# Token weights turned by blocks of rows, and a new order of all steps, in a fused attention and mixing kernel

## The chip, the cores and the metric

The kernel runs on one core of a Trainium2 chip. The core has five engines, each with its own stream of instructions that it works through in order: TensorE (PE; its weight loads are shown apart as PEld), VectorE (DVE), ScalarE (ACT), GpSimd (POOL) and SyncE (SP), which here issues all DMA transfers. Engines wait for each other by semaphores. The metric is device time in microseconds (us) of one execution. The kernel before takes 235.92 us, the median of 3 runs (235.21 to 237.58).

## The reference: what is computed

A block of attention is followed by a block that mixes tokens and channels. Batch 8, heads 8, 576 tokens, 64 features per head; all inputs and the output are float32.

```python
# attention, for each batch and head
q_d, k_d, v_d = means of q, k, v over groups of 4 tokens          # 144 tokens
out_d = softmax(q_d @ k_d.T / 8) @ v_d                             # coarse, all to all
scores = where(|i - j| < 4, q @ k.T / 8, -1e9)                     # local, a band
x = repeat(out_d, 4) + softmax(scores) @ v                         # heads side by side: [8, 576, 512]

# mixing
theta = x @ w_theta
zr, zi = x * cos(theta), x * sin(theta)
y[b] = w_tok_r @ zr[b] + w_tok_i @ zi[b]                           # over the 576 tokens
u = x + y
out = u + maximum(u @ w_ch, 0)
```

## The kernel before, in words

All work is in bfloat16 on the chip, with sums in float32 in PSUM, whose eight banks are one tile `PS`. For each of the 8 batches the steps are, with the two-letter words by which the code names them:

- Loads of q and k (`lq`, `lk`, four pairs of heads each), cast to bfloat16 (`cq`, `ck`, L296), turned on TensorE (`tp`, L303) and evicted from PSUM (`ev`, L316) to `qT` and `kT`. Sums over four tokens give `qd` and `kd` (L322 on VectorE; L330 with L333 or L336 on GpSimd). v comes in windows of 64 tokens (`lv`, `lw`) and is cast (`cv`, L396); v of batch 0 is loaded in rows, cast and turned on the chip (`l1`, `c1`, `t1`, `e1`, `x1`).
- Coarse attention: scores `sd`, exponentials `ed` (L437), product with the means of v `nd`, normalisation `xn` (L457, L458), turn `xd` and copy `xc` (L470) to `xdT`.
- Local attention in units of windows: scores `ps` (L482), exponentials `ex` (L490), a mask `mk` (L501) on VectorE or GpSimd, product with v `po` (L511), normalisation `nm` (L519, L520), turn `xt` (L533), and the sum with the coarse part `xa` (L541), which gives `xT`.
- Mixing: `th` (L552) makes theta for 128 tokens, `cs` (L557, L558) its cosine and sine on ScalarE, `xm` turns x, and `zz` (L616) multiplies x by both to make `z`; the last 64 tokens go another way (`tt`, `ct`, `zt`, `zp`, `zc`, L586). `mx` (L632) is the token mixing, 8 groups of 9 products with a row of 288 columns of `WT`; `ua` (L637) adds x and frees the bank. `ch` (L662) is the channel product, `rl` (L667) its addition and `st` the store.

The token weights must be turned once, at the start, before batch 0 can be mixed. `WT` holds nine pieces of 128 rows (source tokens) by 576 columns (target tokens). `lb` loads nine blocks of rows (four of `w_tok_r`, one that holds the last 64 rows of both, four of `w_tok_i`), `cb` (L261) casts each into a place of `uT`, which is not yet in use, `wp` (L273) turns on TensorE what belongs to one of the nine pieces, from five blocks of one matrix, and `wc` (L278) copies the piece, 576 columns, to `WT`. A piece needs all blocks of its matrix, so the first turn waits for the last block of that matrix.

The order is written out by hand: `ORDER` is one list of words. The first two letters name the step, of which the next instance in a fixed sequence is taken; the third says which engine does it (`v`, `a`, `g`) or which banks or which of the 16 staging places `st` it uses. Each engine gets its instructions in the order of this list, and a chain of no-wait dependencies (`pin`) keeps it so; the engines still drift against each other. `wm` words are dummy products on zeros, placed in the start, and `te` and `ts` load ScalarE's table for exponentials or sines. All transfers stand in one queue, on SP.

## Time and profile before

| | us |
|---|---|
| median of 3 runs (lowest, highest) | 235.92 (235.21, 237.58) |
| span of the profiled execution, first to last instruction | 232.1 |
| median less this span | 3.8 |
| TensorE busy | 220.7 |
| VectorE busy | 191.8 |
| ScalarE busy | 156.1 |
| GpSimd busy | 135.5 |

The profiled execution is shown by its span alone; what lies around the span, the start and the end of the execution, is taken as the difference to the median. Rows of a timeline show start, length, engine, line, operation, output and inputs with their shape, and a count where like instructions follow each other. Rows of a group show the line, engine, operation, tiles, shape and count, then the busy time in us and the mean of one in ns, then the engine's idle time just before them and what ended it. Rows of waits show who waited for whom: us in total, times, and the longest. A matmul's record lasts until its result is out, though the next has begun by then, so TensorE's busy time overstates its work.

The DMA queue and the granted clock in 40 slices of the span, in tenths, for the whole of it:

```
PEclk9999999999999999999999999999999999999998
DMA  6999989999999899989606895899957766556676
```

### The profile page before, as it was taken

The page shows a single profiled execution, that of the slowest core. Times are in us where ns is not written, and L with a number is a line of the kernel's source. Part 1 is how long each engine was busy: PE and PEld are TensorE (multiplying, and loading weights), DVE is VectorE, ACT ScalarE, POOL GpSimd, SP SyncE. Part 2 cuts the span into 40 slices and gives each one's busy share as a digit, 9 for nine tenths or more (in the row PEclk, how much of TensorE's full clock was granted, in tenths as well). Part 3 has the DMA queues.
Part 4 walks back from the last instruction along what each step waited for, and adds up shares of the span by engine and source line. Part 5 has one row for each costly group of instructions (what it writes and reads, how often), then busy time and mean ns, then how long its engine had stood idle before and what let it go on. Part 6 is the DMA issues. An engine that isn't in the chain of part 4 may idle for free.

```text
span 232.1 us, 9462 instructions
## 1 busy us (share of the span) xinstructions
PE 220.7 (95%) x3986; PEld 153.2 (66%) x3986; DVE 191.8 (83%) x365; ACT 156.1 (67%) x241; POOL 135.5 (58%) x179
## 2 busy tenths in 40 slices
PE   7998899999998999999999999999999998999991
PEld 2665678777776765776768766676676563767750
DVE  6699999989997988868997997799889967567572
ACT  3359999799877989867976979857766591620000
POOL 7468989869999656897472837767386510000000
PEclk9999999999999999999999999999999999999998
DMA  6999989999999899989606895899957766556676
GB/s 204 382 392 390 298 134 252 365 263 193 264 263 195 224 290 208 203 209 210 174 3 178 226 234 147 293 249 173 153 122 189 144 138 100 154 126 182 138 235 217
DMA packets 76795, 49.41 MB, mean 213 GB/s; under 512 B 61136, under 2 KB 61392, under 8 KB 76752
## 3 DMA queue, kind: packets, MB, share of 16 engines
q1 hardware_dynamic: 76752, 48.81, 84.6%
q8 instruction: 31, 0.51, 1.1%
q14 instruction: 12, 0.10, 0.2%
HBM read 33.98 MB, written 9.44 MB: 187 GB/s over the span
## 4 chain that ended last, share of the span: by engine, by line
PE 72%; DVE 12%; DMA 5%; SPq 3%; issue 3%; ACT 2%; DVEq 0%
PE PS L632 24%; PE PS L662 10%; PE PS L552 9%; PE PS L303 5%; PE PS L755 4%; PE PS L511 3%; DVE xT L541 3%; DMA out_dram<-osb 2%; DVE pm L501 2%; PE PS L591 2%; PE PS L482 2%; DMA st<-xT 2%; SPq L641 2%; PE PS L533 2%; DVE uT L637 2%
## 5 line engine op out<-in xcount | busy, mean ns | idle before, releaser
L632 PE MATMUL PS<-WT,z 128*128 128x288 bf16 x576 | 77.9, 286 | 1.7 <-issue 1.7
L632 PEld LDWEIGHTS <-z 128*128 128x128 bf16 x576 | 53.8, 98 | 17.5 <-issue 2.8
L637 DVE TENSOR_TENSOR uT<-PS,xT 128x288 bf16<-128x288 f32 x64 | 28.1, 450 | 11.4 <-PE PS L632 11.1
L552 PE MATMUL PS<-wth,xT 128*128 128x512 bf16 x128 | 32.3, 380 | 0.7 <-DVE xT L541 0.7
L557 ACT ACTIVATE cs<-PS,pihc 128x512 bf16<-128x512 f32 x32 | 22.3, 696 | 15.1 <-PE PS L552 9.9
L662 PE MATMUL PS<-wch,uT 128*128 128x512 bf16 (+1 forms) x132 | 30.6, 373 | 0.0
L520 DVE TENSOR_TENSOR tmp<-PS,rl 128x512 bf16<-128x512 f32 x40 | 27.7, 692 | 1.4
L541 DVE TENSOR_TENSOR xT<-PS,xdT 128x928 bf16<-128x928 f32 (+1 forms) x24 | 22.7, 952 | 3.4 <-PE PS L533 3.1
L490 ACT ACTIVATE pm<-PS 128x1024 bf16<-128x1024 f32 (+1 forms) x24 | 20.4, 877 | 7.0 <-PE PS L482 2.7
L501 POOL TENSOR_TENSOR pm<-pm,band 128x1024 bf16<-128x1024 bf16 (+1 forms) x13 | 22.2, 1709 | 2.9 <-ACT pm L490 2.9
L667 DVE SCALAR_TENSOR_TENSOR osb<-PS,ur 128x512 f32<-128x512 f32 (+1 forms) x33 | 21.8, 669 | 2.4 <-PE PS L662 1.6
L330 POOL TENSOR_TENSOR two<-kT 128x580 f32<-128x580 bf16 x15 | 17.5, 1163 | 6.1 <-ACT kT L316 5.2
L296 POOL CAST q_tm<-st 128x576 bf16<-128x576 f32 x22 | 14.4, 664 | 10.8 <-DMA st<-in_q_dram 10.8
L662 PEld LDWEIGHTS <-uT 128*128 128x128 bf16 x132 | 12.2, 98 | 12.2 <-issue 0.3
L558 ACT ACTIVATE cs<-PS 128x512 bf16<-128x512 f32 x32 | 19.4, 605 | 0.0
L330 POOL TENSOR_TENSOR two<-qT 128x576 f32<-128x576 bf16 x11 | 12.8, 1167 | 10.5 <-ACT qT L316 7.1
L552 PEld LDWEIGHTS <-xT 128*128 128x128 bf16 x128 | 11.2, 98 | 10.7 <-issue 1.3
L616 DVE TENSOR_TENSOR z<-PS,cs 128x1024 bf16<-128x1024 bf16 x24 | 16.2, 685 | 1.9 <-PE PS L591 0.9
L437 ACT ACTIVATE pd<-PS 128x864 bf16<-128x864 f32 x16 | 14.1, 889 | 5.2 <-PE PS L426 5.2
L761 ACT ACT_TABLE_LOAD x13 | 16.7, 1283 | 0.2
L296 POOL CAST k_tm<-st 128x576 bf16<-128x576 f32 x21 | 14.4, 695 | 1.4 <-DMA st<-in_k_dram 1.4
L396 POOL CAST v_w<-st 128x512 bf16<-128x512 f32 x21 | 13.3, 653 | 1.3 <-DMA st<-in_v_dram 1.2
(119 smaller groups left out, 419.3 us busy)
## 6 DMA issues: line engine op xcount, KB each, us to landing
st<-in_q_dram SPq DMA_DIRECT2D x32, 288.0 KB, 6.3
st<-in_k_dram SPq DMA_DIRECT2D x32, 288.0 KB, 6.0
st<-in_v_dram SPq DMA_DIRECT2D x70, 128.0 KB, 4.7
out_dram<-osb SPq DMA_DIRECT2D x31, 256.0 KB, 2.9
out_dram<-osb SPq DMA_DIRECT2D x10, 128.0 KB, 2.4
st<-in_v_dram SPq DMA_DIRECT2D x4, 288.0 KB, 3.7
st<-in_moe_w_tok_r_dram SPq DMA_DIRECT2D x4, 288.0 KB, 6.2
st<-in_moe_w_tok_i_dram SPq DMA_DIRECT2D x4, 288.0 KB, 7.2
```

Of the source, the lines that this page charges most:

```text
L296: COPY[w](out=to[:, r, :], in_=of[:, r, :])
L330: nc.gpsimd.tensor_tensor(out=t, in0=src[:, :, 0:2], in1=src[:, :, 2:4], op=ALU.add)
L490: nc.scalar.activation(out=pm[(3 * b + u) % NPM][:, :, 0:n].rearrange("p e c j w -> p e (c j w)"), in_=at.pop(("ps", b, u))[:, :, 0:4 * W ...
L501: EW[w].tensor_tensor(out=t, in0=t, in1=m, op=ALU.mult)
L520: nc.vector.tensor_tensor(out=tmp[(NCH * b + c) % NTMP].rearrange("p g (j d) -> p g j d", d=D), in0=ps[:, :, :, 0:D], in1=r.unsqueeze(3).t ...
L541: nc.vector.tensor_tensor(out=xT[b % 2][:, :, lo:lo + cnt].rearrange("p e (m j) -> p e m j", j=4), in0=at.pop(("xt", b, u))[:, :, 0:cnt].r ...
L552: nc.tensor.matmul(out=ps, lhsT=xT[b % 2][:, dc, P * c:P * c + P], rhs=wth[:, dc, :], start=(dc == 0), stop=(dc == 3))
L557: nc.scalar.activation(out=t[:, 0, :], in_=ps, func=AF.Sin, bias=pihc, scale=1.0)
L632: nc.tensor.matmul(out=ps, lhsT=z[b % 2][:, j, P * dc:P * dc + P], rhs=WT[:, j, cols], start=(j == 0), stop=(j == 8))
L637: nc.vector.tensor_tensor(out=uT[b % 2][:, dc, cols], in0=at.pop(("mx", b, i)), in1=xT[b % 2][:, dc, cols], op=ALU.add)
L662: nc.tensor.matmul(out=ps[:, cols], lhsT=uT[b % 2][:, dc, P * c:P * c + P], rhs=wch[:, dc, cols], start=(dc == 0), stop=(dc == 3))
L667: nc.vector.scalar_tensor_tensor(out=o[:, cols], in0=at["ch", b, c][:, cols], scalar=0.0, in1=ur[b % 2][:, c, cols], op0=ALU.max, op1=ALU.add)
```

## The change

Two things are changed. First, the token weights are turned by blocks of rows (target tokens) and not by pieces of `WT`. `wp(i)` turns block i by itself, five transposes, as soon as this block is cast; `wc(i)` copies the result to columns 128 i to 128 i + 127 of all four pieces of its matrix with one instruction, and the part of the last 64 source tokens with a second one of 64 partitions (for the block that holds the rest of both matrices one and two). The blocks are loaded, cast, turned and copied in the sequence `WTI`, real and imaginary in turn, so that the first 384 columns of `WT` are there after six of nine blocks. The transposes fall from 50 to 45 and the copies rise from 9 to 19, of which 10 are small.

Second, `ORDER` is another list, with other places, other engines for many steps and other banks and staging places. Its words are the same steps, but for one dummy group less, 28 dummy products of 512 columns in place of 40, and 17 loads of ScalarE's table in place of 13. It was laid out with two more rules, that at most eight transfers stand in the queue at a time and that VectorE and GpSimd share a port.

Which engine does a step, counted in the lists (VectorE, ScalarE, GpSimd):

| step | before | after |
|---|---|---|
| casts of k (`ck`) | 1, 10, 21 | 6, 3, 23 |
| casts of q (`cq`) | 0, 10, 22 | 9, 4, 19 |
| casts of v (`cv`) | 8, 11, 21 | 10, 12, 18 |
| evictions of q and k (`ev`) | 9, 21, 2 | 4, 25, 3 |
| sums over q (`qd`) | 5, -, 11 | 1, -, 15 |
| sums over k (`kd`) | 1, -, 15 | 3, -, 13 |
| masks (`mk`) | 11, -, 13 | 12, -, 12 |

```diff
-WPJ = (0, 2, 4, 6, 1, 3, 5, 7, 8)
+WTI = (0, 5, 1, 6, 2, 7, 3, 8, 4)
...
 ORDER = """
-l10 l11 l12 c1v c1a c1g k0 l13 kcv wm061 t101 c1g lq4 e1v wm256 t123 lk5 lk6 kca e1v wm483 x12 x13 lk7 ckv lq8 x10 cka
+kca kcg l10 l11 c1a c1v wm760 t101 l12 l13 c1a c1v e1a lk4 lq5 ckv lq6 lk7 lk8 lk0 wm757 t167 e1a kcg ckv wm552 x17
...
+    def wtb(i):
+        return uT[0][:, i, :] if i < 5 else uT[1][:, i - 5, :]
+
     def cb(i, w):
-        to = uT[0][:, i, :] if i < 5 else uT[1][:, i - 5, :]
-        COPY[w](out=to, in_=at.pop(("wtok", i)))
...
-    def wp(j, w):
-        ps = at["wp", j] = bank16(w)
-        for ri in ((j % 2,) if j < 8 else (0, 1)):
-            lo, n = (0, P) if j < 8 else (HALF * ri, HALF)
-            for ct in ((0, 1, 2, 3, 4), (4, 0, 1, 2, 3))[ri]:
-                base = P * ct - (HALF if ct == 4 and ri else 0)
-                nc.tensor.transpose(out=ps[lo:lo + n, base:base + P],
-                                    in_=(uT[ri][:, ct, :] if ct < 4 else uT[0][:, 4, :])[:, P * (j // 2):P * (j // 2) + n],
-                                    identity=ident)
-
-    def wc(j, w):
-        COPY[w](out=WT[:, j, :], in_=at.pop(("wp", j))[:, 0:S])
+        COPY[w](out=wtb(i), in_=at.pop(("wtok", i)))
+
+    def wp(i, w):
+        ps = at["wp", i] = bank16(w)
+        for c in range(4):
+            nc.tensor.transpose(out=ps[:, P * c:P * c + P], in_=wtb(i)[:, P * c:P * c + P], identity=ident)
+        nc.tensor.transpose(out=ps[:, 512:512 + P], in_=wtb(i)[:, S - P:S], identity=ident)
+
+    def wc(i, w):
+        ps = at.pop(("wp", i))
+        if i == 4:
+            COPY[w](out=WT[:, 0:8, 512:S].rearrange("p (c x) t -> p c x t", x=2),
+                    in_=ps[:, 0:512].rearrange("p (c x t) -> p c x t", x=2, t=HALF))
+            tails = [(ri, 512, HALF * ri, HALF) for ri in range(2)]
+        else:
+            COPY[w](out=WT[:, i // 5:8:2, P * (i % 5):P * (i % 5) + P], in_=ps[:, 0:512].rearrange("p (c t) -> p c t", t=P))
+            tails = [(i // 5, P * (i % 5), 0, P)]
+        for ri, to, of, n in tails:
+            COPY[w](out=WT[HALF * ri:HALF * ri + HALF, 8, to:to + n], in_=ps[HALF:P, 512 + of:512 + of + n])
...
-        wp=(wp, [(j,) for j in WPJ]), wc=(wc, [(j,) for j in WPJ]),
+        wp=(wp, [(j,) for j in WTI]), wc=(wc, [(j,) for j in WTI]),
```

The lines of the steps move by five (L296 to L301, L541 to L546, L616 to L621, L632 to L637, L637 to L642).

Three places show what the new list does. The first is ScalarE at the beginning (rows: line, operation, output and inputs with shape, count; `z_103` is z of batch 0, which holds v rows at that time, `pu` the selection of means, `xT_102` holds the turned v). Before:

```order
L372 CAST z_103<-st 128x9x64
L231 COPY pu_133<-full_137 64x32 x2
L296 CAST k_tm_74<-st 128x9x64
L296 CAST q_tm_77<-st 128x9x64
L394 CAST v_w_70<-PS 128x8x64 x2
L296 CAST k_tm_75<-st 128x9x64
L296 CAST q_tm_78<-st 128x9x64
L316 COPY kT_62<-PS 128x2x576
L316 COPY qT_64<-PS 128x1152
```

After:

```order
L231 COPY pu_132<-full_136 64x32 x2
L377 CAST z_103<-st 128x9x64 x2
L385 COPY xT_102<-PS 128x1152 x2
L399 CAST v_w_70<-PS 128x8x64 x3
L321 COPY kT_62<-PS 128x2x576
L321 COPY qT_64<-PS 128x1152
L321 COPY kT_62<-PS 128x2x576
L321 COPY qT_64<-PS 128x1152
```

ScalarE has lost the casts of batch 0's q and k, and has got the evictions of turned v and all four evictions of q and k of batch 0, of which VectorE had two.

The second place is VectorE ahead of the first mixing (`z_103` with `cs_105` to `cs_108` are the four products of batch 0, the copy to `z_103` is its tail). Before:

```order
L616 TENSOR_TENSOR z_103<-PS,cs_105 128x1024
L278 COPY WT<-PS 128x576
L616 TENSOR_TENSOR z_103<-PS,cs_106 128x1024
L616 TENSOR_TENSOR z_103<-PS,cs_107 128x1024
L322 TENSOR_REDUCE qd_69<-qT_65 128x288
L278 COPY WT<-PS 128x576 x6
L616 TENSOR_TENSOR z_103<-PS,cs_108 128x1024
L586 COPY z_103<-PS 128x512
```

After:

```order
L280 COPY WT<-PS 128x4x128
L283 COPY WT<-PS 64x128
L621 TENSOR_TENSOR z_103<-PS,cs_106 128x1024
L280 COPY WT<-PS 128x4x128
L283 COPY WT<-PS 64x128
L578 TENSOR_TENSOR zT<-xT_101,cst 128x512
L280 COPY WT<-PS 128x4x128
L283 COPY WT<-PS 64x128
L621 TENSOR_TENSOR z_103<-PS,cs_107 128x1024
L591 COPY z_103<-PS 128x512
L621 TENSOR_TENSOR z_103<-PS,cs_108 128x1024
```

The copies to `WT` now stand between the products, the sum over q is no longer on this engine here, and the fourth product closes the row.

The third place is VectorE a little later, while batch 0 is mixed (`uT` is u of batch 0, `xdn` the coarse attention of batch 1, `tmp` its local attention, `q_tm` q of batch 2). Before:

```order
L637 TENSOR_TENSOR uT_111<-PS,xT_101 128x288
L519 RECIPROCAL rl_94<-PS 128x8
L520 TENSOR_TENSOR tmp_89<-PS,rl_94 128x512
L637 TENSOR_TENSOR uT_111<-PS,xT_101 128x288
L457 RECIPROCAL rd_97<-PS 72x8
L458 TENSOR_TENSOR xdn_96<-PS,rd_97 72x512
L457 RECIPROCAL rd_98<-PS 72x8
L458 TENSOR_TENSOR xdn_96<-PS,rd_98 72x512
```

After:

```order
L642 TENSOR_TENSOR uT_111<-PS,xT_101 128x288
L301 CAST q_tm_78<-st 128x8x64
L301 CAST q_tm_78<-st 128x64
L462 RECIPROCAL rd_97<-PS 72x8
L463 TENSOR_TENSOR xdn_96<-PS,rd_97 72x512
L462 RECIPROCAL rd_98<-PS 72x8
L463 TENSOR_TENSOR xdn_96<-PS,rd_98 72x512
```

A cast of q, in two instructions, has come onto VectorE between an addition into u and the normalisation; another stands between the two sums into `xT` that follow.

More of the change, by code (lines that the diff above doesn't have):

```diff
@@ new lines @@
+x16 lq9 kcg x10 cva cva x11 x12 cvv cva tp34 eva lq1 cvv lk2 ckv ckv cqg cqg cqg lb3 tp67 eva cqv pv01 wm512 tp23 qdg
+eva kdv kdg wm513 tp67 eva wm552 ps67 vdv ps45 cka lk4 qdv wm354 sd01 ex sd67 mkv lk5 la6 la7 ex po45 po23 cbg mkv lba
+nm nm la0 ed la9 ed ckg tp01 eva cbg nd67 cag cag nd45 xn lk1 cag po01 lq8 caa lqb lb2 ps23 lbc cqg ex mkg lq3 wp6 xn
+po23 lb4 lba cqg wca xd4 wp5 nm nm xt67 xca xa po01 wca cbg xt23 kdg xa lq6 lb0 ckg tp45 evv ckg cba ts th7 cs wp6 cqg
+cqg th2 cs th3 nm cs xm7 xt01 wcv tp45 xa lb9 lb8 lvb lvc lw cbg wp6 lv2 tt0 zz wp3 wcv lv1 xm7 lv3 zz lw lw lw lw
@@ L97 @@
+ua zz st rl ch0 ua utg dt ua dz cs zz zz ht5 rt ss zz mx7 ua sr mx1 ua mx6 mx5 mx7 mx1 mx2 ua ua ua mx7 ua mx1 mx6 mx5
+mx4 mx3 st rl ua st ua ua ch7 ua ua ua ch4 du ch5 ch6 ch2 ch1 ua du du du rl rl st du du ch7 ch0 uta du du st utg dt
+st rl st rl rl rl rl ht1 st st rm st st su rl st rt sr ss k0
 """
@@ L711 @@
     STEPS = dict(
-        k0=(lambda i, w: None, span(1)), kc=(kc, span(4)), la=(la, span(4)), ca=(ca, span(4)), lb=(lb, span(9)), cb=(cb, span(9)), lc=(lc, span(4)), cc=(cc, span(4)),
-        wp=(wp, [(j,) for j in WPJ]), wc=(wc, [(j,) for j in WPJ]),
+        k0=(lambda i, w: None, span(1)), kc=(kc, span(4)), la=(la, span(4)), ca=(ca, span(4)), lb=(lb, [(i,) for i in WTI]), cb=(cb, [(i,) for i in WTI]), lc=(lc, span(4)), cc=(cc, span(4)),
+        wp=(wp, [(j,) for j in WTI]), wc=(wc, [(j,) for j in WTI]),
         lk=(load(0), span(B, 4)), lq=(load(1), span(B, 4)), ck=(cast(0), span(B, 4)), cq=(cast(1), span(B, 4)),
```

70 lines of the change are left out of this document (31 added, 39 removed).

## The prediction

> **What bounds the kernel now.** I read the page first, then the busy time by stretch, the timelines of single engines, the groups by shape and the waits. The page:
>
> ```profile
> span 232.1 us, 9462 instructions
> PE 220.7 (95%) x3986; PEld 153.2 (66%) x3986; DVE 191.8 (83%) x365; ACT 156.1 (67%) x241; POOL 135.5 (58%) x179
> ```
>
> TensorE is busy for 95% of the span. The share is an average over unlike stages, so I cut the span where the token mixing (L632) of batch 0 begins, where that of batch 5 begins, and at the end. TensorE's timeline has these places:
>
> ```profile
> 37.26 2.37 PE L632 MATMUL PS<-WT,z 128*128 128x288 bf16 x18
> 168.63 3.48 PE L632 MATMUL PS<-WT,z 128*128 128x288 bf16 x27
> 219.10 7.08 PE L662 MATMUL PS<-wch,uT 128*128 128x512 bf16 x36
> ```
>
> Busy time by stretch (length, busy and count of PE, PEld, DVE, ACT, POOL, then granted clock, DMA share, GB/s):
>
> ```profile
> 0.00:20.00 20.00, 18.74 (x232) 10.28 (x233) 15.84 (x40) 9.69 (x15) 13.16 (x35) 1.00 0.93 334
> 20.00:37.30 17.30, 15.55 (x422) 12.26 (x421) 16.79 (x34) 17.24 (x27) 15.25 (x19) 1.00 0.97 246
> 37.30:60.60 23.30, 23.26 (x492) 17.90 (x490) 21.79 (x38) 20.95 (x35) 19.69 (x24) 1.00 1.07 267
> 168.80:199.70 30.90, 29.52 (x518) 18.55 (x517) 26.21 (x46) 17.94 (x28) 12.66 (x14) 1.00 0.65 136
> 37.30:168.80 131.50, 129.51 (x2629) 93.42 (x2627) 113.93 (x210) 107.78 (x168) 94.44 (x111) 1.00 0.93 216
> 168.80:232.10 63.30, 56.86 (x710) 37.25 (x708) 45.27 (x84) 21.37 (x34) 12.66 (x14) 0.99 0.65 159
> ```
>
> Three stages with different limits are to be seen. In the start (0 to 37.3) TensorE mostly fills time with dummy products; from 20 us on VectorE (16.79 of 17.30) and ScalarE (17.24 of 17.30) are full and set the pace. In the middle (131.5 us) TensorE is idle for 131.50 - 129.51 = 2.0 us by these rows, and VectorE has 131.50 - 113.93 = 17.6 us to spare. The end (63.3 us) has TensorE again as the limit, but for 1.4 us in the stretch 168.8 to 199.7 and what comes after 219.10 + 7.08 = 226.2, when only the shared tail product and stores are left. So the change can win in the start, and in the middle it can mainly lose.
>
> **Start: the fourth product.** Mixing of batch 0 needs four z products of VectorE and the copied tail. The timelines of VectorE, ScalarE and GpSimd before it:
>
> ```profile
> 32.42 1.30 DVE L616 TENSOR_TENSOR z<-PS,cs 128x1024 bf16<-128x1024 bf16 x2
> 33.64 1.34 DVE L322 TENSOR_REDUCE qd<-qT 128x288 bf16<-128x1152 bf16 x1
> 34.90 2.27 DVE L278 COPY WT<-PS 128x576 bf16<-128x576 bf16 x6
> 37.08 0.68 DVE L616 TENSOR_TENSOR z<-PS,cs 128x1024 bf16<-128x1024 bf16 x1
> 37.68 0.42 DVE L586 COPY z<-PS 128x512 bf16<-128x512 bf16 x1
> 34.58 0.67 ACT L558 ACTIVATE cs<-PS 128x512 bf16<-128x512 f32 x1
> 32.69 0.67 POOL L261 CAST uT<-st 128x576 bf16<-128x576 f32 x1
> ```
>
> The sines for the fourth product are ready at 34.58 + 0.67 = 35.25, but VectorE makes it at 37.08, because six copies of token weights (2.27 us) and a sum over q (1.34) stand ahead. They stand there because GpSimd's last cast of token weights ends only at 32.69 + 0.67 = 33.36. In the changed order (the rows on VectorE that are shown with the change) the sum over q has gone to GpSimd, and six of nine blocks are copied ahead of the fourth product, between the others; they hold the columns that the first four mixings read. Three blocks are copied behind it. The sixth block's cast stands three casts ahead of GpSimd's last, so 3 x 0.67 = 2.0 us sooner, near 31.4, which is early enough.
>
> I take the fourth product at 35.25, when its sines are ready as before: 37.08 - 35.25 = 1.8 us earlier. ScalarE was full in this stretch (17.24 of 17.30) and has the same amount ahead of these sines, so it gives little; it starts sooner on the evictions of batch 0, which all four stand on it now, and I add 0.3 for that: **start 37.3 - 2.1 = 35.2**. Bounds: 0 (the copies come late all the same) and 4 (ScalarE gains two us as well). Twelve dummy products of 512 columns fewer cost nothing: they fill TensorE's waits for casts and evictions, and those set the pace there with or without them. Five transposes fewer lie under the same cover. SP issues 233 transfers in both kernels; the last load of token weights is the 34th in both, and that of theta the 21st in place of the 23rd, so no load of batch 0 is pushed behind more bytes.
>
> **Middle: VectorE fills up.** The instructions on each engine between the first mixing of batch 0 and that of batch 5, counted in the order of both kernels, by the rows of the groups by shape:
>
> ```profile
> L296 DVE CAST k_tm<-st 128x512 bf16<-128x512 f32 x1 | 0.4, 427 | 0.0
> L296 DVE CAST k_tm<-st 128x64 bf16<-128x64 f32 x1 | 0.2, 189 | 0.0
> L396 DVE CAST v_w<-st 128x512 bf16<-128x512 f32 x5 | 4.1, 826 | 0.0
> L316 DVE COPY qT<-PS 128x1152 bf16<-128x1152 bf16 x3 | 4.1, 1355 | 0.6 <-PE PS L303 0.5
> L501 DVE TENSOR_TENSOR pm<-pm,band 128x1024 bf16<-128x1024 bf16 x9 | 11.0, 1217 | 0.0
> L501 DVE TENSOR_TENSOR pm<-pm,band 128x512 bf16<-128x512 bf16 x2 | 1.2, 622 | 0.0
> L519 DVE RECIPROCAL rl<-PS 128x8 f32<-128x8 f32 x40 | 8.0, 199 | 1.1 <-PE PS L511 0.8
> L520 DVE TENSOR_TENSOR tmp<-PS,rl 128x512 bf16<-128x512 f32 x40 | 27.7, 692 | 1.4
> L541 DVE TENSOR_TENSOR xT<-PS,xdT 128x928 bf16<-128x928 f32 x16 | 17.9, 1121 | 3.4 <-PE PS L533 3.1
> L649 DVE COPY ur<-PS 128x512 bf16<-128x512 bf16 x6 | 2.4, 417 | 0.8 <-PE PS L646 0.8
> L761 ACT ACT_TABLE_LOAD x13 | 16.7, 1283 | 0.2
> L761 ACT ACTIVATE idle<-pihc 128x1 f32<-128x1 f32 x13 | 2.6, 203 | 0.1
> ```
>
> VectorE gains ten casts of q and k (10 x (0.427 + 0.189) = 6.2 us), four of v (3.3), two sums into xT (2.2), two normalisations (2 x 0.891 = 1.8), three row copies (1.25), half a mask (0.6) and small ones (net 1.2, at some 0.4 each as the row copy); it loses three evictions (-4.1) and two full masks (-2.4). Net +10.0: 113.9 + 10.0 = 123.9 us. Part of this is only moved ahead from the end. TensorE's own middle grows by two score units and one turn of batch 6, by these pieces of the chain of waits 2 x 0.39 + 0.37 = 1.1 us, which the end loses:
>
> ```profile
> 49.69 0.37 PE PS L533 x32
> ...
> 99.71 0.39 PE PS L482 x32
> ```
>
> ScalarE gets four table loads more (4 x (1.283 + 0.203) = 5.9), three evictions and two exponentials more and ten casts and copies fewer, some +8 together: 116 of 131. GpSimd gets three masks (2.12 each, row below), five sums over q and one eviction more and six q casts and four small ones fewer, some +12: 107 of 131. Neither is the limit.
>
> Of the table loads the Trainium skill (ScalarE: Activation LUTs, What ACT_TABLE_LOAD costs) says that a switch costs some 2.66 us, since a drain of 1.38 us follows the load; by it the four more would cost ScalarE 10.6 us in place of 5.9. The rows above leave 0.1 us of idle time behind 13 loads together, so no such drain shows here and I use the rows.
>
> VectorE works in order, so a cast that waits for its load holds all behind it. The second place shown with the change is such: in batch 0's mixing two casts of q now stand ahead of the normalisation of batch 1's coarse attention, and two more inside the sums into xT. Behind them wait the additions into uT (L637, L642 after), and for these TensorE, whose banks they free. How full can VectorE be? The fullest stretch where it sets the pace is 16.79/17.30 = 97.1%; in the fullest where TensorE does, 21.79/23.30 = 93.5%. The casts are new neighbours of GpSimd's work, and on this point the timelines show a lock:
>
> ```profile
> 19.97 0.69 DVE L501 TENSOR_TENSOR pm<-pm,band 128x1024 bf16<-128x1024 bf16 x1
> 130.87 2.12 POOL L501 TENSOR_TENSOR pm<-pm,band 128x1024 bf16<-128x1024 bf16 x1
> 131.61 1.93 DVE L501 TENSOR_TENSOR pm<-pm,band 128x1024 bf16<-128x1024 bf16 x1
> ```
>
> The same mask takes 0.69 us alone and 1.93 beside GpSimd's: it ends 0.55 after GpSimd's ends (132.99 to 133.54). A cast of 128x512 costs 0.427 clear and 0.826 on average for v: 0.40 of waiting. Between none and all (10 x 0.40 = 4.0) I take half, 2.0: 125.9 us of work, which is 129.7 at 97.1% and 134.7 at 93.5%, on the mean 132.2. TensorE alone gives 131.5 + 1.1 = 132.6, if it idles as before. **Middle: 132.2**, 0.7 longer. The ends are 130.6 (TensorE without its 2.0 us of idle) and rival 4.
>
> **End.** 63.3 - 1.1 (moved ahead) - 0.4 (of the 1.4 us of idle, as the front work of batches 6 and 7 lies further ahead) = **61.8**. The last steps are the same chain: the channel products, the shared tail product, its addition and its stores.
>
> **Sum.** 35.2 + 132.2 + 61.8 = 229.2 against a span of 232.1. The median of the runs is 235.92, so 3.8 us lie around the span: 229.2 + 3.8 = **233.0 us**, 1.2% below before. A measurement of this kernel can tell about 1% from no change, so the bounds are 233.6 and 238.3.
>
> **Rivals.**
> 1. *TensorE alone limits the middle.* The layout keeps VectorE's casts clear of GpSimd, and the middle falls to 129.5 + 1.1 = 130.6: 231.4 us. For it: 17.6 us of VectorE's idle time. Against: 10 of these are filled.
> 2. *The start is not gained; turning by rows does not do what it says.* All nine turns still stand ahead of the first mixing on TensorE, so no mixing begins before the last block is cast and turned. GpSimd has as much ahead of its last token cast as before, and if that slips past 35 the last turn holds TensorE. Then 37.3 + 132.2 + 61.8 + 3.8 = 235.1, no change. Against it: 33.36 leaves 1.8 us.
> 3. *A late load stops VectorE.* The waits show what a load can do to an engine that casts:
>
> ```profile
> POOL q_tm L296 <- DMA st<-in_q_dram: 10.8, 4, 5.3
> DVE uT L637 <- PE PS L632: 11.1, 15, 2.4
> ```
>
> GpSimd waited 10.8 us in four waits, the longest 5.3. One mean wait of 2.7 that nothing covers gives 235.7, the longest 238.3: no change. Against it: the 11.1 us in which VectorE waited for mixing are cover.
> 4. *The lock decides (slower).* GpSimd is busy for 107 of 131 us, 81%, and each of its instructions takes 94.44/111 = 0.85 us. If each of the 24 pieces added (20 of q and k, four of v) meets it at that rate and waits half an instruction, 24 x 0.81 x 0.43 = 8.4 us come on top of 123.9: 132.3, at 93.5% a middle of 141.5, and 35.2 + 141.5 + 61.8 + 3.8 = 242.3. It decides where the middle passes 137.5, which is 128.6 us of work or 4.7 of waiting. Against it: VectorE's masks and v casts paid such waits before, and two masks fewer pay them now. The Trainium skill (SBUF — State Buffer, SBUF: two separate sides) states such a rule: VectorE, in a two-port mode or with two inputs in SBUF, and GpSimd share one port pair as an exclusive lock, held for a whole instruction, and the loser stands still. By that rule, the trace's masks at 130.87 and 131.61 agree.
>
> **How the numbers follow.** The forecast 0.33 and rival 1 0.11 make faster 0.44; rival 2 0.19 and rival 3 0.14 make the same 0.33; rival 4 makes slower 0.23. The range: rival 1 with half a gain more at the start (231.4 - 2.4) below, 229.0; above, rival 4 only to where a third of it is in, 239.0. The forecast's own range is 231 to 235.
>
> **What would show it.** The first mixing starts near 35 us, with the fourth z product close behind its sines (right), or at 37 with weight copies ahead of it (rival 2). VectorE in the middle is busy for about 125 us with casts near 0.43 and 0.19 for the small piece (forecast), or over 129 with casts at 0.8 and more that end just behind GpSimd's instructions (rival 4). VectorE's waits list loads of q or k for under 3 us (forecast) or over 5 (rival 3). The prediction is wrong if TensorE shows idle time over 5 us in the middle that ends on none of these, for instance on SP's queue.

## The result: 252.8 us, 7% slower

The changed kernel takes 252.82 us, the median of 4 runs (250.65 to 254.02); the kernel before, on the same chip, 235.56 (234.45 to 237.58). The ratio is 1.070 (95% interval 1.060 to 1.080). Now and then an execution of a kernel, the kernel before among them, runs in a slower state of the chip; medians here and below include such runs and ratios do not, so a ratio can differ from that of two medians. The profiled execution took 254.02 (the longest of the four), of which 252.3 are the span. From its page, the span, the busy time of each engine and the granted clock in 40 slices:

```profile
span 252.3 us, 9404 instructions
PE 221.6 (88%) x3940; PEld 154.5 (61%) x3967; DVE 204.4 (81%) x396; ACT 161.2 (64%) x247; POOL 139.0 (55%) x177
PEclk9999999999999999999997999999999999889997
```

TensorE has the work it had (221.6 us against 220.7) in a span that is 20 us longer. (The 17 us between the medians are less, since the profiled execution of the kernel before was shorter than its median and this one is longer than its own.) Cut where the mixing of batch 0 begins, where that of batch 5 begins, and at the end, the busy times are (columns as in the prediction):

```profile
0.00:35.37 35.37, 30.76 (x629) 21.27 (x634) 29.52 (x77) 29.62 (x43) 28.78 (x57) 1.00 0.94 307
35.37:186.01 150.64, 133.73 (x2706) 96.25 (x2721) 133.95 (x243) 113.09 (x174) 101.60 (x113) 0.99 0.76 192
186.01:252.30 66.29, 57.07 (x617) 36.94 (x614) 40.98 (x78) 18.51 (x31) 8.60 (x9) 0.95 0.56 144
```

The start is 35.4 us (predicted 35.2), the middle 150.6 (132.2), the end 66.3 (61.8). In the middle TensorE is idle for 150.64 - 133.73 = 16.9 us, where it was 2.0 before, and VectorE's busy time has grown from 113.9 to 133.95. By the waits of TensorE in this stage, some 13 of the 16.9 us ended with an instruction of VectorE.

**The start came out as predicted.** Timelines of VectorE, ScalarE and TensorE ahead of the first mixing:

```profile
33.68 0.69 DVE L621 TENSOR_TENSOR z<-PS,cs 128x1024 bf16<-128x1024 bf16 x1
34.62 0.68 DVE L621 TENSOR_TENSOR z<-PS,cs 128x1024 bf16<-128x1024 bf16 x1
33.61 0.68 ACT L563 ACTIVATE cs<-PS 128x512 bf16<-128x512 f32 x1
35.37 0.90 PE L637 MATMUL PS<-WT,z 128*128 128x288 bf16 x6
```

The fourth z product starts 0.33 us behind its sines (33.61 + 0.68 = 34.29) and the first mixing follows at 35.37. No other profile of a kernel with the new list starts so early (table below).

**The middle lost to waits inside VectorE's instructions.** VectorE's groups by shape:

```profile
L401 DVE CAST v_w<-st 128x512 bf16<-128x512 f32 x8 | 8.4, 1059 | 0.0
L301 DVE CAST q_tm<-st 128x64 bf16<-128x64 f32 x9 | 7.4, 821 | 0.0
L506 DVE TENSOR_TENSOR pm<-pm,band 128x1024 bf16<-128x1024 bf16 x8 | 7.3, 935 | 0.0
L301 DVE CAST q_tm<-st 128x512 bf16<-128x512 f32 x9 | 7.2, 803 | 0.0
...
L301 DVE CAST k_tm<-st 128x512 bf16<-128x512 f32 x6 | 2.9, 489 | 1.8 <-DMA st<-in_k_dram 1.7
L301 DVE CAST k_tm<-st 128x64 bf16<-128x64 f32 x6 | 2.1, 344 | 0.0
```

A piece of 64 elements of q takes 821 ns on average, as long as one of 512 (803); clear they took 189 and 427. Over the 15 casts this is 9 x (0.376 + 0.632) + 6 x (0.062 + 0.155) = 10.4 us of waiting. One place shows how it comes about; timelines of GpSimd, VectorE and TensorE:

```profile
160.66 2.39 POOL L318 COPY kT<-st 128x1152 bf16<-128x1152 bf16 x1
162.99 2.33 POOL L318 COPY qT<-st 128x1152 bf16<-128x1152 bf16 x1
161.86 3.52 DVE L301 CAST q_tm<-st 128x512 bf16<-128x512 f32 x2
165.52 0.69 DVE L525 TENSOR_TENSOR tmp<-PS,rl 128x512 bf16<-128x512 f32 x1
166.27 1.02 PE L637 MATMUL PS<-WT,z 128*128 128x288 bf16 x7 [2.81 <-DVE tmp L525]
```

The row of VectorE holds both pieces of one cast. They end at 161.86 + 3.52 = 165.38, which is 0.06 after GpSimd's second copy ends (165.32). That is 2.9 us more than a clear pair (0.62), longer than what was left of the first copy (163.05 - 161.86 = 1.2): the pair met two GpSimd instructions. The normalisation behind it came late, and TensorE stood for 2.81 us.

**The end.** Timelines of SP (transfers as they are issued), VectorE and TensorE:

```profile
212.22 3.83 SPq L606 DMA_TRANSPOSE st<-xT  x3
216.11 2.03 SPq L676 DMA_DIRECT2D out_dram<-osb  x4
218.18 1.37 SPq L606 DMA_TRANSPOSE st<-xT  x1
218.46 0.69 DVE L672 SCALAR_TENSOR_TENSOR osb<-PS,ur 128x512 f32<-128x512 f32 x1 [4.17 <-DMA out_dram<-osb]
223.06 0.69 DVE L616 TENSOR_TENSOR z<-st,cs 128x1024 bf16<-128x1024 bf16 x1 [3.55 <-issue]
219.20 2.32 PE L637 MATMUL PS<-WT,z 128*128 128x288 bf16 x9 [2.46 <-DVE osb L672]
```

An addition of batch 5 waits 4.17 us for a store that stands behind three transposes of batch 7's xT, and the first z of batch 7 starts 3.5 us after the fourth, which stands behind four stores, was issued. Here the profile names no releaser for that z; in stores_last and more_osb below it names this transpose. TensorE waits for the addition, and the granted clock is down to 0.95 in this stage.

### The profile page after: what moved, and what is told of

Its sections match the earlier page's. It is cut to its first block, busy times and chain, and to the rows that moved or that the text cites. A ratio compares the mean times of both kernels' runs of the same rounds, so it can differ in the third digit from the quotient of the medians.

```text
span 252.3 us, 9404 instructions
## 1 busy us (share of the span) xinstructions
PE 221.6 (88%) x3940; PEld 154.5 (61%) x3967; DVE 204.4 (81%) x396; ACT 161.2 (64%) x247; POOL 139.0 (55%) x177
## 4 chain that ended last, share of the span: by engine, by line
PE 49%; DVE 21%; issue 8%; DMA 8%; POOL 5%; SPq 4%; ACT 3%; DVEq 0%; POOLq 0%; ACTq 0%
PE PS L637 20%; PE PS L667 7%; PE PS L557 6%; DMA st<-in_k_dram 4%; DVE q_tm L301 3%; DVE pm L506 3%; DVE xT L546 2%; PE PS L308 2%; DVE v_w L401 2%; DMA st<-in_v_dram 2%; PE PS L516 2%; DVE tmp L525 2%; DVE osb L672 2%; SPq L606 1%; DMA st<-in_q_dram 1%
## 5 line engine op out<-in xcount | busy, mean ns | idle before, releaser
L637 PE MATMUL PS<-WT,z 128*128 128x288 bf16 x576 | 80.1, 291 | 10.8 <-DVE uT L642 3.4
L637 PEld LDWEIGHTS <-z 128*128 128x128 bf16 x576 | 55.3, 99 | 28.6 <-issue 12.8
L642 DVE TENSOR_TENSOR uT<-PS,xT 128x288 bf16<-128x288 f32 x64 | 28.2, 450 | 11.1 <-PE PS L637 10.7
L557 PE MATMUL PS<-wth,xT 128*128 128x512 bf16 x112 | 30.1, 379 | 1.6 <-DVE xT L546 0.7
L335 POOL TENSOR_TENSOR two<-kT 128x580 f32<-128x580 bf16 x13 | 15.9, 1220 | 15.3 <-ACT kT L321 14.9
L335 POOL TENSOR_TENSOR two<-qT 128x576 f32<-128x576 bf16 x15 | 18.2, 1212 | 10.5 <-ACT qT L321 10.2
L546 DVE TENSOR_TENSOR xT<-PS,xdT 128x928 bf16<-128x928 f32 (+1 forms) x24 | 22.3, 951 | 1.7 <-PE PS L538 1.1
L621 DVE TENSOR_TENSOR z<-PS,cs 128x1024 bf16<-128x1024 bf16 x24 | 16.1, 682 | 2.5 <-ACT cs L563 1.4
L301 POOL CAST k_tm<-st 128x576 bf16<-128x576 f32 x23 | 16.7, 741 | 1.2 <-DMA st<-in_k_dram 1.2
L657 POOL COPY ut<-uT 128x256 bf16<-128x256 bf16 x5 | 2.0, 400 | 26.7 <-DVE uT L642 26.7
L321 ACT COPY qT<-PS 128x1152 bf16<-128x1152 bf16 x12 | 13.6, 1133 | 3.8 <-PE PS L308 3.8
```

Source lines behind the costliest of these rows:

```text
L301: COPY[w](out=to[:, r, :], in_=of[:, r, :])
L335: nc.gpsimd.tensor_tensor(out=t, in0=src[:, :, 0:2], in1=src[:, :, 2:4], op=ALU.add)
L546: nc.vector.tensor_tensor(out=xT[b % 2][:, :, lo:lo + cnt].rearrange("p e (m j) -> p e m j", j=4), in0=at.pop(("xt", b, u))[:, :, 0:cnt].r ...
L557: nc.tensor.matmul(out=ps, lhsT=xT[b % 2][:, dc, P * c:P * c + P], rhs=wth[:, dc, :], start=(dc == 0), stop=(dc == 3))
L637: nc.tensor.matmul(out=ps, lhsT=z[b % 2][:, j, P * dc:P * dc + P], rhs=WT[:, j, cols], start=(j == 0), stop=(j == 8))
L642: nc.vector.tensor_tensor(out=uT[b % 2][:, dc, cols], in0=at.pop(("mx", b, i)), in1=xT[b % 2][:, dc, cols], op=ALU.add)
```

## The experiments

The table has, for each kernel, the median, its ratio to the kernel before in the same set of runs (that one moves between 235.6 and 239.4 us from set to set, so compare ratios), and from one profiled execution the three stages as cut above and VectorE's busy time in the middle. Stages carry some uncertainty: two kernels with the same program up to batch 5 had middles of 150.6 and 145.4 (changed and stores_early), the 12 kernels with the new list have starts of 35.4 to 37.5, all but the changed one from 36.3 on, and kernels with the old order and turning have 37.3 to 38.9. Stages of before_split are left out, since its profiled execution was its longest (245.2). Numbers of lines shift by a few between these kernels.

| kernel | us | ratio (95%) | start | middle | end | VectorE in the middle, if used |
|---|---|---|---|---|---|---|
| before | 235.6 | 1 | 37.3 | 131.4 | 63.5 | 114.0 |
| changed | 252.8 | 1.070 (1.060 to 1.080) | 35.4 | 150.6 | 66.3 | 134.0 |
| rows_only | 238.2 | 1.011 (1.001 to 1.021) | 39.0 | 133.9 | 63.8 | 115.6 |
| whole_casts | 244.2 | 1.036 (1.028 to 1.044) | 36.5 | 139.8 | 66.0 | 124.8 |
| casts_act | 245.0 | 1.038 (1.031 to 1.045) | 36.3 | 140.8 | 66.6 | 118.4 |
| stores_early | 251.2 | 1.062 (1.051 to 1.074) | 36.9 | 145.4 | 65.5 | 131.0 |
| pool_halves | 248.2 | 1.049 (1.036 to 1.063) | 36.9 | 144.2 | 66.2 | 129.0 |
| before_split | 242.0 | 1.023 (1.011 to 1.035) | - | - | - | - |
| before_whole | 239.5 | 1.013 (0.999 to 1.027) | 38.9 | 135.4 | 63.8 | - |
| whole_v_act | 241.2 | 1.021 (1.011 to 1.032) | 36.3 | 137.5 | 65.6 | 118.0 |
| whole_v_halves | 240.8 | 1.017 (1.012 to 1.023) | 36.4 | 136.0 | 66.5 | 117.4 |
| end_order | 244.8 | 1.033 (1.027 to 1.039) | 36.9 | 138.0 | 70.0 | - |
| all_three | 243.0 | 1.026 (1.019 to 1.032) | 37.5 | 136.1 | 68.8 | - |
| more_osb | 241.3 | 1.019 (1.015 to 1.024) | 37.0 | 136.7 | 66.2 | - |
| before_halves | 236.1 | 0.996 (0.989 to 1.003) | 38.6 | 131.4 | 62.9 | 111.1 |
| stores_last | 237.5 | 1.004 (1.001 to 1.008) | 37.1 | 136.7 | 62.3 | 118.2 |
| last_act | 239.3 | 1.015 (1.009 to 1.021) | 36.4 | 138.6 | 62.4 | 111.4 |

### rows_only: the turning by rows under the old order

```diff
 ORDER = """
-kca kcg l10 l11 c1a c1v wm760 t101 l12 l13 c1a c1v e1a lk4 lq5 ckv lq6 lk7 lk8 lk0 wm757 t167 e1a kcg ckv wm552 x17
...
+l10 l11 l12 c1v c1a c1g k0 l13 kcv wm061 t101 c1g lq4 e1v wm256 t123 lk5 lk6 kca e1v wm483 x12 x13 lk7 ckv lq8 x10 cka
...
```

> The list of steps of before, with the token weights loaded, cast, turned and copied by blocks of rows. If the turning by rows costs (ten small copies more, strided writes), some 2 us more than before (238). If the loss lies in the new list alone, as I hold: the time of before within 1%, 233 to 238, with VectorE's weight copies near 0.42 and 0.23 us. Where the lock or the loads are the cause, this run shows no loss.

Measured: 1.1% above before. On VectorE's timeline the fourth z product starts only behind all the row copies:

```profile
39.21 0.40 DVE L283 COPY WT<-PS 64x64 bf16<-64x64 bf16 x2
39.64 0.69 DVE L621 TENSOR_TENSOR z<-PS,cs 128x1024 bf16<-128x1024 bf16 x1
```

So the new turning by itself costs about a per cent (0.1 to 2.1) and gains no start; the gain in the start needs the order that puts six copies between the products, and most of the 7% comes with the new order.

### whole_casts: VectorE's casts of q and k as one instruction

```diff
-            for r in ((slice(0, WR - 1), slice(WR - 1, WR)) if w == "v" else (slice(0, WR),)):
-                COPY[w](out=to[:, r, :], in_=of[:, r, :])
+            COPY[w](out=to, in_=of)
```

> The changed kernel, with each cast of q or k on VectorE made by one instruction of 128x9x64 in place of 128x8x64 and 128x64. The work, its place, its loads and its buffers are the same. Lock theory: an odd count of rows leaves no two-port mode, the cast takes about 0.66 us, holds no port and waits for none: the mean falls from 1.62 (0.803 + 0.821 for q) to about 0.7, VectorE's busy time by some 10 us, and the time by 6 to 12 us (241 to 247). Theory that late loads and staging places set the middle: the casts still wait for data and the time stays within 2 us of 252.8. If the whole cast takes the lock as well, but once: half the gain, 3 to 5 us.

Measured: 3.4 points of ratio come back, some 8 us, and the intervals are apart. The rows of the casting line, with min/median/max in ns:

```profile
L300 DVE CAST q_tm<-st x9: 733/743/744, 13.2 to 154.9; 128x576 bf16<-128x576 f32 x9
L300 DVE CAST k_tm<-st x6: 739/744/754, 7.7 to 124.8; 128x576 bf16<-128x576 f32 x6
```

All 15 take 0.73 to 0.75 us, whatever GpSimd does. The cast of q that took 3.52 us in two pieces beside GpSimd's copies shows it; it now lies wholly within the first of these copies:

```profile
153.75 2.38 POOL L317 COPY kT<-st 128x1152 bf16<-128x1152 bf16 x1
154.94 0.73 DVE L300 CAST q_tm<-st 128x576 bf16<-128x576 f32 x1
```

The order, the loads and the casts' places are the same, so the waits of the pieces cost this much and not the loads that the casts wait for. Clear, the pair is cheaper (0.62 against 0.74).

### casts_act: the ten casts from the first mixing on given to ScalarE

```diff
-cqv ... ckv
+cqa ... cka
```

> The changed kernel, with the ten casts of q and k that VectorE makes from the first mixing on moved to ScalarE, at the same places of the list. Lock theory: VectorE loses its waits and 6 us of work, ScalarE (112 of 149 us in the middle) takes 10 x 0.68 us: 238 to 244. Load alone (VectorE merely has 6 us too much): about 6 us less, 246 to 248. Theory of late loads: ScalarE waits in place of VectorE, 250 to 254.

Measured: the same gain by another way (245.0 against 244.2). VectorE's middle is 6.4 us lighter than with whole casts (118.4 against 124.8), and the time is not better. That the load of these casts on VectorE cost nothing beyond the waits is not shown by this: TensorE now waits 2.7 us for casts of q on ScalarE, which may hide a gain.

### pool_halves: GpSimd's masks in two halves

```diff
+        if w == "g" and n == 2:
+            for y in range(2):
+                nc.gpsimd.tensor_tensor(out=t[:, 8 * y:8 * y + 8], in0=t[:, 8 * y:8 * y + 8], in1=m[:, 8 * y:8 * y + 8], op=ALU.mult)
+            return
         EW[w].tensor_tensor(out=t, in0=t, in1=m, op=ALU.mult)
```

> The changed kernel with each of GpSimd's masks of 128x1024 written as two instructions of 128x512, so that GpSimd never holds longer than about 1.1 us at a time; VectorE's instructions are untouched. Lock theory: VectorE waits to the end of one GpSimd instruction, so the longest waits (casts, half masks and zT at 2 us and more) are halved; VectorE's busy time in the middle falls from 134 to 128 to 131 and the kernel from 252.8 to 246 to 250. Rival, order or loads: GpSimd does the same work with a few more instructions, 252 to 254 us.

Measured: 248.2 us, in the range of the lock theory: 2.1 points below the changed kernel and 1.3 below stores_early, which has the same program up to batch 5. The intervals overlap in both cases, so the gain is not settled. No instruction of VectorE was touched; its busy time in the middle is 129.0, against 134.0 and 131.0 in those two. GpSimd's copies of 128x1152 (2.3 us) were not cut, and beside them the same cast of q still takes 3.49 us.

### before_split and before_whole: the ten casts put into the kernel before

```diff
-cqg ... ckg
+cqv ... ckv
```

Ten casts of GpSimd (six of q, four of k) go to VectorE in the old order, once in pieces and once whole.

> The kernel before, with ten of the 36 casts of q and k that GpSimd does between the first mixing of batch 0 and that of batch 5 given to VectorE at the same places of the order, each in two pieces (128x512 and 128x64). Nothing else of the change is in it. Lock theory: VectorE's pieces stand still beside GpSimd's instructions (in the changed kernel a pair took 1.6 us where it needs 0.62 clear), so the ten pairs take 10 to 18 us of VectorE in place of 6.2 and the kernel ends at 239 to 246 us; single pieces over 1.5 us are seen. Rival, plain load: ten pairs of 0.62 fit into the 17.4 us that VectorE has to spare in the middle, and GpSimd gets 6 us less: 235 to 237 us. Rival, order: the loss of the changed kernel is in its order alone, and this one is also at 235 to 237.

> The same ten casts given to VectorE in the kernel before, but each as one instruction of 128x9x64, which took 0.74 us wherever GpSimd was in the changed kernel. Lock theory: 10 x 0.74 = 7.4 us of VectorE without waits, 234.5 to 238 us, 3 to 8 us below the kernel with the pieces. Rival, late loads: the casts stop VectorE because their loads are late and not because of GpSimd, then both forms are equally slow, within 1.5 us of each other, and the waits list loads of q or k on VectorE for over 3 us.

Measured: ratios of 1.023 and 1.013, with medians of 242.0 and 239.5 us. Rows of the casting line, pieces first (from its longest execution, so they show that pieces wait and not how much they cost), whole below:

```profile
L303 DVE CAST q_tm<-st x12: 189/416/1140, 45.5 to 172.5; 128x512 bf16<-128x512 f32 x6, 128x64 bf16<-128x64 f32 x6
...
L303 DVE CAST k_tm<-st x10: 184/623/2108, 10.2 to 139.3; 128x512 bf16<-128x512 f32 x5, 128x64 bf16<-128x64 f32 x5
```

```profile
L302 DVE CAST q_tm<-st x6: 742/744/746, 43.5 to 166.6; 128x576 bf16<-128x576 f32 x6
...
L302 DVE CAST k_tm<-st x5: 737/744/753, 9.9 to 135.0; 128x576 bf16<-128x576 f32 x5
```

The pieces wait here too, up to 2.1 us, and the order of the two kernels is as the lock theory says. The sizes were off: the pieces cost 1.0 points, some 2.4 us, more than whole casts (expected 3 to 8), and the intervals overlap. Whole casts are not shown to be free either: 1.3% above before, with an interval that just holds 1.

### whole_v_act: the later casts of v given to ScalarE too

In the kernel with whole casts TensorE's idle stretches still stood behind VectorE instructions that had been held, by its timelines:

```profile
161.99 2.59 DVE L400 CAST v_w<-st 128x512 bf16<-128x512 f32 x2
164.50 0.68 DVE L671 SCALAR_TENSOR_TENSOR osb<-PS,ur 128x512 f32<-128x512 f32 x1
165.23 0.38 PE L650 MATMUL PS<-ident,uT 128*128 128x128 bf16 x4 [1.51 <-DVE osb L671]
```

```diff
-cvv
+cva
```

> The changed kernel with whole casts of q and k (244.2 us so far) and with the seven casts of v that VectorE makes after the first mixing given to ScalarE. Theory that the lock also explains the rest: in the kernel with whole casts the idle stretches of TensorE still stand behind VectorE instructions that were held (two casts of v in 2.59 us, a half mask of 2.32, a zT of 1.28); without the casts of v some 6 us of VectorE's work and 3 of waiting go, and 240 to 242.5 us are left. Rival, order: VectorE was busy 89% of that middle, so its load is not what holds, 243.5 to 245.5.

Measured: 241.2 us, 1.5 points less, in the range of the lock theory, with intervals that just overlap. This edit takes work and waiting away together, so by itself it doesn't tell them apart.

### stores_early and end_order: two orders of SP's queue in the end that did not help

stores_early is the changed kernel with the four stores of batch 4 each behind its addition; end_order is whole_v_act with the same and with batch 7's four transposes put right behind its xT.

```diff
-... xa dz tt0 ch6 ch7 zz zz cs zz du du th4 zz mx2 dx3 ct ztg th0 dx dx1 rl st st st st rl th5 rl cs mx1 mx6 dx cs
+... xa dx3 dx dx5 dx dz tt0 ch6 ch7 zz zz cs zz du du th4 zz mx2 ct ztg th0 rl st rl th5 rl cs mx1 mx6 cs
```

> The changed kernel, with the four stores of batch 4 that stand on SP behind three transposes of batch 7 put right behind their additions. If these stores hold the output buffers, and so VectorE (4.17 us of waiting for a store at 218) and the mixing of batch 6: 3 to 5 us less (248 to 250). If the chain of transposes on SP sets the end by itself: less than 1 us.

> The same kernel without the halves, with the end of SP's order changed: each of the four stores of batch 4 right behind its addition, and the four transposes of batch 7's xT right behind the addition that fills it (in stage places 3 and 5), ahead of two transposes of batch 5's uT. Theory: in the end TensorE waits 2 to 2.5 us for an addition that waits for a store behind these transposes, and the granted clock falls after it; with both in time the end goes from 65.7 to 61 to 63.5 us and the kernel to 236.5 to 239.5. Rival: SP has the same transfers to issue at some 1.3 us for each transpose, and what comes sooner for batch 7 comes later for batch 5's rows; the end stays within 1.5 us and the kernel at 240 to 242.

Measured: stores_early gave 0.7 points, with intervals that overlap, and the wait for the stores became one for the fourth transpose. end_order made the end longer, 70.0 us against 65.6. The tail's transpose for batch 6 (`dz`) now stood behind four transposes, and by the waits on TensorE the mixing of batch 6 stopped for it:

```profile
PE PS L643 <- DMA z<-zT: 4.0, 1, 4.0
```

My theory of the right order was wrong, and its rival (what comes sooner for one comes later for another) understated it.

### whole_v_halves and all_three

> The changed kernel with whole casts of q and k, the seven later casts of v on ScalarE (241.2 us together) and GpSimd's full masks in two halves. Lock theory: VectorE's masks of 128x512 (0.96 us on average, 0.41 clear) and zT (0.55, 0.41 clear) are the last that wait, some 3 to 5 us together with the full masks; the middle goes from 137.5 to 135 to 136.5 and the kernel to 239 to 240.5. Rival, the rest is order: 241 to 242.5.

> Both edits together. If they add up, 234.5 to 238.5 us, level with the kernel before; if the lock and the end's queue are not the causes, 240 to 242.

Measured: GpSimd's masks in halves bring the middle from 137.5 to 136.0, as expected, but 0.4 points of the whole with overlapping intervals: not settled. all_three has the wrong end in it: 68.8 us.

### more_osb and stores_last: the additions freed from the stores, then the stores moved

In more_osb (on whole_v_halves) the eight sums of batches 4 and 5 go to stage places that no load uses any more. stores_last has in addition five stores behind batch 7's transposes.

```diff
+    OPL = (0, 2, 4, 5, 6, 7, 9, 11)
+
+    def otile(b, c):
+        if b in (4, 5):
+            return stg[OPL[4 * (b - 4) + c]][:, 0:DM]
+        return osb[(4 * b + c + b // 2) % NOSB]
...
-dx dx1 rl st st st st rl th5 rl cs mx1 mx6 dx cs ua zz st rl ch0 ua utg dt ua dz cs zz
+dx dx1 rl rl th5 rl cs mx1 mx6 dx cs ua zz rl ch0 ua utg dt ua dz st st st st st cs zz
```

> The changed kernel with whole casts, v on ScalarE and halved GpSimd masks (240.8 us), and the output sums of batches 4 and 5 written to eight stage places that no load uses any more, in place of the five places for sums, so that no such addition waits for a store. SP's order stays. Theory: the 2.5 us of TensorE's idle time ahead of batch 6's second mixing, and the fall of the granted clock behind it (1.7 us), come from additions that wait for stores; the end goes from 66.5 to 62.5 to 64 us and the kernel to 237 to 239. Rival: SP's queue of transposes is what holds the end (the rows of batch 5 come late all the same), the wait of the addition turns into one for its row transposes or for batch 7's, and 240 to 241.5 are left.

> As more_osb (241.3 us), but the five stores that stand between and behind batch 7's transposes on SP come behind the transpose of its tail (dz); no addition waits for them. Theory: SP's queue holds the end. The fourth transpose of batch 7 is issued 2.7 us sooner, VectorE's first z of batch 7 starts near 207 in place of 209.6, TensorE's wait of 3.8 us falls under 1.5 and the granted clock stays at 1.00; the end goes from 66.2 to 62 to 64 us and the kernel to 237 to 239.5. Rival: the transposes that remain in the queue (four of batch 7, two of batch 5) set the end by themselves, 65 to 66 us and 240 to 241.5.

Measured, more_osb: the waits for stores are gone and the end is still 66.2 us. Its timelines of SP, VectorE and TensorE:

```profile
203.59 2.70 SPq L693 DMA_DIRECT2D out_dram<-st  x4
206.33 1.44 SPq L616 DMA_TRANSPOSE st<-xT  x1
209.64 0.69 DVE L626 TENSOR_TENSOR z<-st,cs 128x1024 bf16<-128x1024 bf16 x1 [7.03 <-DMA st<-xT]
210.99 13.22 PE L647 MATMUL PS<-WT,z 128*128 128x288 bf16 x93 [3.81 <-DVE st L689]
```

So the rival was right: VectorE now waits 7.03 us for the fourth transpose, which was issued behind four stores. stores_last moves only these stores:

```profile
199.46 5.93 SPq L616 DMA_TRANSPOSE st<-xT  x4
...
206.80 1.22 SPq L592 DMA_TRANSPOSE z<-zT  x1
208.07 2.78 SPq L693 DMA_DIRECT2D out_dram<-st  x5
206.69 0.69 DVE L626 TENSOR_TENSOR z<-st,cs 128x1024 bf16<-128x1024 bf16 x1 [4.31 <-DMA st<-xT]
208.04 8.25 PE L647 MATMUL PS<-WT,z 128*128 128x288 bf16 x66 [0.52 <-DVE st L689]
```

VectorE starts batch 7's z 2.95 us sooner and TensorE waits 0.52 us in place of 3.81; the end is 62.3 us and the kernel 237.5, level with before (1.004). The queue's order set the end.

### before_halves and last_act: does waiting or load on VectorE cost where it has time?

before_halves is the kernel before with GpSimd's full masks in halves and its four later casts of v on ScalarE; last_act is stores_last with ten casts of q and k on ScalarE.

> The kernel before with GpSimd's full masks in two halves and its four later casts of v on ScalarE. Theory that the lock costs only where VectorE has no time to spare: VectorE's waiting in the middle falls by 3 us or more, but TensorE is idle for only 2.0 of 131.4 us there, so the kernel stays within 1.5 us of before. Rival, the lock costs wherever it is met: 2 to 4 us faster.

> As stores_last (237.5 us), with the ten casts of q and k that VectorE makes from the first mixing on given to ScalarE. Load theory: the middle is still 136.7 us against 131.4 before because VectorE (118.1 us busy) holds TensorE in short waits; without 7.4 us of casts its work is below that of the kernel before, the middle falls to 132.5 to 135 and the kernel to 233.5 to 236, ahead of both. Rival, the order of steps itself: the middle stays at 136 to 138 though VectorE is less busy, and 237 to 239 are left.

Measured: before_halves is level with before (0.996, interval across 1) with a middle of 131.4 us again, as expected. But the test is weak: VectorE's busy time in the middle fell only from 114.0 to 111.1, of which 4 x 0.427 = 1.7 us are the plain work of the four casts, so little waiting was taken away (expected 3 us or more). last_act fell on the rival's side, and was slower than stores_last. The middles of stores_last and last_act:

```profile
37.08:173.76 136.68, 131.64 (x2723) 94.63 (x2721) 118.17 (x226) 115.39 (x179) 98.28 (x118) 1.00 0.83 211
```

```profile
36.39:175.02 138.63, 130.72 (x2707) 94.76 (x2721) 111.38 (x216) 120.66 (x189) 97.85 (x118) 1.00 0.82 208
```

With VectorE less busy than in the kernel before (111.4 against 114.0) the middle is still 138.6. So VectorE's amount of work is not what makes this middle longer than 131.4. But the edit moved a wait as well; the longest of TensorE's waits in last_act is one for a cast on ScalarE that stores_last has not:

```profile
PE PS L314 <- ACT q_tm L307: 1.8, 1, 1.8
```

It is about as long as the middle of last_act is longer (1.9), so what less load on VectorE would be worth without it is not shown. In stores_last, TensorE's own work is 2.3 us more than before (131.64 against 129.38, where the prediction had 1.1), partly steps that the new order brings forward from the end; some 3 us of idle time are in short waits that I did not trace to one cause. That stays open. No kernel here is shown to beat the one before.

## Why the prediction was wrong

**The start (35.2, measured 35.4) was right** in place and in mechanism. That it agrees to 0.2 us is partly luck: the other kernels with the new list start at 36.3 to 37.5, and other profiles of the old order at 38.6 and 38.9, so the gain of about 2 us is what is borne out. Terms cancel, too: the sines were ready 1.0 us sooner (34.29 after 35.25) and not 0.3, but the first mixing followed the start of the fourth product by 0.75 us and not by 0.18 as before. Rival 2 did not come, but rows_only (39.0) shows that the turning by itself gains no start.

**VectorE's plain work was right.** I counted 123.9 us without waits of the ten new casts. With whole casts, which cost 10 x (0.744 - 0.616) = 1.3 us more and don't wait, it was 124.8, against 125.2 by that count.

**The step that failed is the waiting at the lock**: "Between none and all (10 x 0.40 = 4.0) I take half, 2.0". Measured are 10.4 us on the casts of q and k. Two things were wrong with it. The 4.0 was no upper bound: it charged each cast once with the mean wait of a v cast, though a cast is two instructions and each can wait for the rest of a GpSimd instruction, up to 2.1 us in this trace. And the small piece was priced at 189 ns, as if too short to meet anything; it waited longest. Rival 4 counted 24 pieces and 8.4 us and had the mechanism and VectorE's work (132.3, measured 133.95); I gave it 0.23. The Trainium skill (SBUF — State Buffer, section SBUF: two separate sides), which rival 4 named, says that the loser of the lock stands still for the whole of the other's instruction; the pair that ends 0.06 us behind GpSimd's copy agrees. Why the whole cast never waits the trace doesn't show. The Trainium skill (VectorE: DVE Perf Modes, section What auto-detection actually checks) lets a copy take the mode with two ports only where the outermost dimensions of source and destination are both even or equal. The whole cast writes nine rows that lie apart and reads nine rows that touch. If these count as nine on both sides, they are equal, and the page would allow two ports; if the source counts as one run of 576, it would not. No run here tells which, but the steady 0.74 us, slower than the clear pair, fits a mode with one port.

**The fill was the second error.** I turned VectorE's work into time at a fill of 93.5 to 97.1%. It was 133.95/150.64 = 88.9%, and last_act's middle at 111.4/138.6 = 80% shows that fill is no property of the stage. A held cast delays the step behind it that frees a bank, and TensorE, which had only 2.0 us to spare, stands still, for 3.09 and 2.81 us at the longest. By the working of rival 4 the middle would have been 141.5; it was 150.6. Rival 3 was not the cause: VectorE's one wait for a load of k, 1.7 us, lay in the start, and in the middle it waited for no load.

**The end (61.8, measured 66.3) failed at "The last steps are the same chain".** I compared the chain of work and not SP's queue: the new order puts four stores among batch 7's transposes, and the additions and z products wait on both sides of them. With five stores moved and the additions freed it was 62.3, 0.5 from the figure predicted.

**The sum of the misses** against the profiled execution: start 0.2, middle 18.4, end 4.5, less 2.1 because only 1.7 us (not 3.8) lay around its span (the 3.8 compared the span of a short execution with the median of others), 21.0 us from 233.0 to 254.0. In points of ratio the way back from 1.070 goes by 3.4 (waits of the casts of q and k), 1.5 (casts of v, waits and work, with intervals that just overlap), 0.4 (GpSimd's masks, not settled) and 1.3 (the end: the stores in SP's queue, and the additions freed from them), to 1.004.

## What to carry to other kernels

An instruction that can be locked out by another engine is priced per instruction and not per step, with the other engine's longest instruction as the bound: cut it in two and it can wait twice. One slower form that did not wait here (0.74 us) was worth more than a faster pair (0.62) that did. In the old order, where VectorE had time to spare, the ten casts cost 2.3% in pieces and 1.3% whole (the latter not shown to differ from nothing), a third and less of the 7%. When an order is moved, read the queue of transfers at the end as an engine of its own: which transpose stands behind which store decided 4 us.

## What was not expected of the hardware

The granted clock fell after short idle stretches of TensorE. Busy time and clock (third column from the right) of the changed kernel in 10 us around its waits of 3.09, 2.81 and 2.46 us:

```profile
130.00:140.00 10.00, 7.19 (x93) 4.49 (x94) 8.09 (x14) 3.71 (x7) 7.83 (x11) 0.83 0.83 213
163.00:173.00 10.00, 7.14 (x90) 4.77 (x89) 9.44 (x17) 6.71 (x12) 7.11 (x7) 1.00 0.59 162
214.00:224.00 10.00, 7.22 (x33) 3.75 (x33) 2.29 (x5) 2.27 (x5) 0.00 (x0) 0.83 0.74 196
```

At the first and the last the clock lost 10 x 0.17 = 1.7 us of work, at the second none, so the length of the wait alone doesn't decide. stores_early says it more sharply: TensorE waits 3.08 us at the instruction where the changed kernel waits 3.09, and its clock stays at 1.00 there.

In slices of 0.5 us the two falls run from 133.64 to 137.05 and from 218.97 to 222.38, each 3.41 us at half the clock, and their starts are 85.33 us apart, which is 25 times 3.41. This suggests, from few cases, that the clock is set at a fixed beat. In the beat that ended where the clock fell, TensorE had stood still for 2.4 and 2.2 us; the waits of 2.81 and 3.08, by the same beat counted on (in stores_early from its fall at 219.64), fell across two beats, with at most 1.9 us in one.

Where it falls, a wait of 2.5 to 3 us costs half as much again and more. With the end's order mended, the page of stores_last shows the clock at nine tenths or more in all slices but the last:

```profile
PEclk9999999999999999999999999999999999999996
```
